# A retention layer and a channel mix on one core: scaled shifted rows on ScalarE instead of a difference on VectorE for four blocks, and a new hand-set order

## The chip, the core and the metric

The kernel runs on one core of one Trainium2 chip. A core has five engines that run side by side, each with its own queue of instructions taken strictly in order: PE (TensorE, matrix multiplication; PEld are its weight loads), DVE (VectorE), ACT (ScalarE), POOL (GpSimd, here used only to issue DMAs) and SP (SyncE, likewise). The metric is the device time of one execution in microseconds (us); less is better.

## The reference

Two layers, float32 in and out, batch B=4, heads H=8, tokens S=768, head size D=64, so the model width is 512; the hidden width of the second layer is 1024.

```
for t in range(S):
    state = gamma[None, :, None, None] * state + einsum('bhd,bhe->bhde', k[:, :, t], v[:, :, t])
    y[:, :, t] = scale * einsum('bhd,bhde->bhe', q[:, :, t], state)
...
x = y with the heads side by side; x_prev = x shifted by one token (a zero row first)
xk = mu_k * x + (1.0 - mu_k) * x_prev
xr = mu_r * x + (1.0 - mu_r) * x_prev
k = maximum(xk @ w_k, 0.0)
v = k * k @ w_v
r = 1.0 / (1.0 + exp(-(xr @ w_r)))
out = r * v
```

## The kernel before, in words

The 4 x 768 tokens are 12 blocks of 256 tokens, numbered 0 to 11; three of them make one batch row. Each block goes through two halves.

The first half is the retention in chunked form. `lq`, `lk`, `lv` load q, k and v of a block (`load`, lines 223 to 238); q and k are turned to fp16 on the way when POOL issues the load, while the very first loads of block 0 go over SP in fp32 and are cast on ACT (`cq`, `ck`). `vs` scales v on DVE (line 254). `Tq` and `Tk` transpose q and k on PE (line 273 for blocks 0 to 5, line 279 for blocks 6 to 11) and ACT copies them out of PSUM (`Eq`, `Ek`, line 242). `S` makes the scores on PE, `M` masks them on DVE (lines 348 and 355). `C` makes the block's part of the state on PE, `U` adds it up (DVE, line 420; the first of a batch row is a copy on ACT or DVE, lines 242 and 244), and `G` decays it into the next block (ACT as four instructions, line 425, or DVE as one, line 429). `I`, `Y` and `J` add the three parts of y on PE, and `D` writes y, transposed and scaled, into the tile `xT` on DVE (lines 508 and 515).

The second half is the channel mix. `dx` (line 530) takes on DVE the difference of the rows of `xT` and the rows shifted by one token, for the whole block: 1024 elements in each of 128 partitions. `X.n.w.j` (line 539) makes a quarter j of the mixed rows on DVE: difference times mu plus the shifted rows, once for the keys (w=0) and once for the gate (w=1), 256 elements for a single block and 512 for a pair. `K` multiplies the mixed rows by w_k on PE (line 563 for single blocks, line 553 for the pairs 3+4, 6+7 and 9+10), ACT takes the result out of PSUM (`Qa`, relu, line 572) and squares it (`Qb`, lines 580 and 584). `R` is the gate's product on PE (line 593) and `s` the sigmoid on ACT (line 599). `V` multiplies the squares by w_v (line 605), `O` multiplies by the gate on DVE (line 611), and `st` stores over SP.

The weights are loaded by POOL in halves: `wk.1` and `wk.0` (line 700), `wr` (line 703), `wv.0` and `wv.1` (line 707). `z.c` are matrix multiplications of zeros that fill PE's waits near the start (c // 4 of them in fp32, line 668, and c % 4 in fp16, line 675).

Nothing schedules this at run time. The string `ORDER` (lines 23 to 75) lists every piece in order, and each engine issues its own pieces in just this order. After `@` stand the PSUM banks of a piece, after `~` its engine or its DMA queue (v is DVE, a ACT, p POOL, s SP). A piece waits until what it reads has been written and until the bank or buffer that it writes has been read. Of the tiles for v there are four, so that the loads of blocks 0 to 3 wait for no one. DVE's first pieces in ORDER, once y of block 0 is there, are

```
D.0~v ... U.1.0 ... dx.0~v X.0.0.0 ... M.1.1~v M.1.0~v ... X.0.0.3 ... X.0.0.2 ... X.0.0.1 D.1~v
```

Of the kernel before, what the change touches and what calls it, by code (L numbers as in the profile page):

```python
# [28 lines left out]
z.4@2 S.1.1@01 lk.2~p I.1@45 S.1.0@23 M.1.1~v M.1.0~v lq.2~p Tq.2@6 Eq.2~a wk.1~p X.0.0.3 Tk.2@0
X.0.0.2 z.1@1 Y.1 J.1 X.0.0.1 D.1~v U.1.1 Ek.2~a z.1@2 S.2.1@01 S.2.0@23 K.0.2@6 dx.1~v K.0.3@4  # L30
Qa.0.3 Qa.0.2 wk.0~p z.2@5 K.0.1@7 Qa.0.1 K.0.0@5 Qb.0.2 X.0.1.0 X.1.0.2 lv.2~p Qa.0.0 Qb.0.1
X.1.0.3 wr~p X.1.0.1 X.1.0.0 K.1.2@4 lv.3~p G.1~a K.1.1@7 X.0.1.1 vs.2~v Qa.1.2 Qb.1.2 M.2.1~v
Qb.0.0 C.2@5 U.2.0 K.1.0@6 lq.3~p Qa.1.1 X.0.1.2 X.0.1.3 K.1.3@0 Qa.1.3 I.2@45 R.0.1@1 R.0.0@7
s.0.1 M.2.0~v Y.2 Qa.1.0 X.1.1.3 X.1.1.2 Qb.1.0 Tq.3@1 Eq.3~a J.2 X.1.1.0 X.1.1.1 R.1.0@6 s.0.0
lk.3~p Tk.3@1 vs.3~v D.2~v dx.2~v X.2.0.2 X.2.0.0 C.3@23 X.2.0.3 Ek.3~a s.1.0 X.2.0.1 lk.4~p
U.3.0~a R.1.1@0 lq.4~p s.1.1 Tk.4@1 S.3.1@45 S.3.0@67 Qb.1.1 Qb.1.3 U.3.1 lv.4~p Tq.4@0 Ek.4~a
Eq.4~a wv.0~p K.2.2@2 Qa.2.2 M.3.1~v K.2.0@3 Qa.2.0 G.3~a M.3.0~v K.2.3@1 vs.4~v Qb.0.3 S.4.1@45
S.4.0@67 M.4.0~v I.3@23 M.4.1~v Qa.2.3 lq.6~p lq.7~p K.2.1@0 Qb.2.0 Y.3 C.4@67 V.1.0.0@1 U.4.0
U.4.1 G.4~a I.4@45 J.3 Qa.2.1 D.3~v dx.3~v Y.4 V.1.1.0@6 Tq.7@23 J.4 D.4~v wv.1~p Qb.2.1
V.0.1.0@0 lk.6~p V.0.0.0@7 X.2.1.2 dx.4~v X.3.0.1 X.3.0.2 X.3.0.3 Eq.7~a V.1.1.1 X.3.0.0 V.0.0.1  # L40
O.0.0 Tk.6@45 Ek.6~a lq.5~p Tq.6@23 lv.5~p Qb.2.2 V.0.1.1 Eq.6~a V.1.0.1 O.1.0 K.3.6@4 K.3.1@5
Qb.2.3 lk.5~p K.3.0@7 Qa.3.6 Tq.5@4 Qa.3.1 Qa.3.0 vs.5~v C.5@5 X.2.1.1 Eq.5~a Tk.5@1 Ek.5~a
S.6@23 O.0.1 O.1.1 lk.7~p U.5.0 Tk.7@67 Ek.7~a X.2.1.0 I.5@45 M.6~v X.3.1.3 K.3.2@0 K.3.3@1
Qa.3.2 Qb.3.1 lv.6~p S.5.0@23 Qa.3.3 Qb.3.0 X.3.1.1 S.5.1@67 Qb.3.3 X.2.1.3 Qb.3.2 K.3.4@0
st.0.0 Qa.3.4 M.5.1~v lk.8~p K.3.5@1 Qa.3.5 R.2.1@6 lv.8~p lk.9~p s.2.1 M.5.0~v Y.5 S.7@23
Tk.8@01 Ek.8~a J.5 X.3.1.0 X.3.1.2 R.3.1@7 s.3.1 V.2.0.0@6 K.3.7@0 lv.7~p vs.6~v R.2.0@7 V.2.0.1
D.5~v M.7~v s.2.0 dx.5~v X.5.1.1 O.2.0 Qa.3.7 Qb.3.6 V.2.1.0@1 Tk.9@23 C.6@45 U.6.0~a Ek.9~a
lq.8~p Tq.8@67 Qb.3.7 X.5.0.3 V.2.1.1 vs.7~v R.4.0@0 Eq.8~a U.6.1 U.6.2 X.5.0.0 U.6.3 st.0.1
R.3.0@2 C.7@45 X.5.0.1 s.4.0 I.6@67 s.3.0 st.1.1 X.5.0.2 K.5.3@3 Qa.5.3 O.2.1 lq.10~p K.5.1@0
Qa.5.1 G.6~v X.5.1.3 V.3.0.0@1 U.7.0 U.7.1 U.7.2 st.2.1 I.7@23 Y.6 vs.8~v U.7.3 G.7~a lq.11~p  # L50
R.4.1@0 D.6~v V.4.1.0@4 lv.11~p C.8@67 Y.7 V.3.1.0@5 Qb.5.1 Qb.3.4 Qb.3.5 V.3.0.1 dx.6~v s.4.1
U.8.0 U.8.1 V.3.1.1 Qb.5.3 D.7~v U.8.2 V.4.1.1 dx.7~v X.6.0.1 X.6.0.3 V.4.0.0@7 K.5.0@6 X.5.1.2
X.6.0.2 Qa.5.0 V.4.0.1 Qb.5.0 K.5.2@0 X.6.0.0 Qa.5.2 Qb.5.2 X.6.1.2 lv.9~p K.6.7@6 Qa.6.7 st.2.0
st.1.0 O.4.1 O.3.0 K.6.0@2 Qa.6.0 lk.10~p O.4.0 O.3.1 st.3.1 K.6.4@0 S.8@67 I.8@23 Tk.10@45
Qa.6.4 K.6.1@1 Ek.10~a X.6.1.1 X.5.1.0 Qa.6.1 Qb.6.1 K.6.6@0 Qb.6.0 Qa.6.6 vs.9~v K.6.5@4 Qa.6.5
M.8~v R.5.1@1 Qb.6.6 Tq.10@67 Eq.10~a s.5.1 Y.8 Tq.11@45 Qb.6.7 lv.10~p vs.10~v X.6.1.3 Eq.11~a
D.8~v dx.8~v lq.9~p X.8.0.2 X.8.0.1 lk.11~p R.5.0@0 s.5.0 K.6.3@6 Qa.6.3 V.5.1.0@7 Tq.9@23
X.6.1.0 Eq.9~a S.10@45 M.10~v Qb.6.3 C.9@01 U.9.0~v st.3.0 U.9.1 V.5.1.1 K.6.2@6 Qa.6.2 R.6.1@2
s.6.1 U.9.2 R.6.0@3 s.6.0 I.9@45 U.9.3 O.5.1 X.8.0.3 S.9@01 M.9~v X.8.0.0 G.9~a C.10@67 U.10.0
U.10.1 Qb.6.2 vs.11~v R.7.1@2 s.7.1 V.5.0.0@3 Qb.6.5 st.4.1 Tk.11@01 Ek.11~a U.10.2 U.10.3  # L60
V.5.0.1 Qb.6.4 K.8.0@2 Qa.8.0 G.10~v I.10@01 Y.9 C.11@67 st.4.0 R.7.0@2 O.5.0 V.6.1.0@3 D.9~v
U.11.0 U.11.1 s.7.0 K.8.3@4 Qa.8.3 V.6.1.1 U.11.2 I.11@67 st.5.0 dx.9~v O.6.1 S.11@45 X.8.1.2
Y.10 V.7.1.0@2 M.11~v D.10~v dx.10~v X.9.0.3 X.9.0.2 X.9.0.1 V.7.0.0@3 Y.11 X.9.0.0 Qb.8.0
K.8.2@4 Qa.8.2 X.8.1.0 X.9.1.1 K.8.1@5 Qa.8.1 D.11~v V.6.0.0@0 V.7.0.1 V.6.0.1 K.9.3@1 K.9.7@5
Qa.9.7 X.8.1.1 V.7.1.1 X.8.1.3 dx.11~v K.9.2@4 O.7.0 Qb.8.1 Qb.9.7 O.6.0 Qa.9.3 st.5.1 Qa.9.2
X.11.1.0 Qb.8.3 X.11.0.3 K.9.1@5 K.9.4@6 st.7.0 Qa.9.1 Qb.9.1 R.8.0@1 s.8.0 V.8.1.0@3 Qb.9.2
X.9.1.0 K.9.0@0 Qa.9.0 Qb.8.2 X.9.1.2 Qb.9.3 K.9.6@1 Qa.9.6 Qb.9.6 O.7.1 st.7.1 K.9.5@7 Qa.9.5
V.8.0.0@0 X.11.0.2 X.11.0.1 Qb.9.0 X.11.0.0 K.11.3@2 K.11.0@1 Qa.11.3 st.6.1 R.8.1@5 V.8.1.1
X.11.1.2 Qa.9.4 st.6.0 X.9.1.3 R.9.1@2 R.10.1@4 R.10.0@6 V.8.0.1 O.8.0 s.8.1 K.11.1@5 Qb.9.4
s.10.0 V.9.0.0@7 V.9.1.0@0 Qa.11.1 Qb.11.1 O.8.1 Qb.9.5 Qb.11.3 Qa.11.0 st.8.1 K.11.2@6 Qa.11.2  # L70
V.10.1.0@5 Qb.11.2 Qb.11.0 V.9.1.1 R.9.0@1 X.11.1.3 s.9.0 X.11.1.1 V.9.0.1 O.9.0 st.9.0
V.11.0.0@6 s.10.1 s.9.1 O.9.1 st.9.1 V.10.0.0@1 V.10.1.1 O.10.1 st.8.0 st.10.1 V.11.0.1 R.11.0@0
s.11.0 O.11.0 V.10.0.1 R.11.1@7 s.11.1 O.10.0 st.10.0 Vc.11.1.1@0 Oc.11.1.1 Vc.11.1.0@6 st.11.0
sc.11.1.1~a Oc.11.1.0 sc.11.1.0~s
"""


# [687 lines left out]
```

## Time and profile before

| | us |
|---|---|
| median of 3 runs (156.35, 156.45, 157.85) | 156.45 |
| the profiled execution | 156.1 |
| its span in the trace | 154.3 |
| busy: PE / DVE / ACT / POOL | 147.3 / 128.1 / 99.1 / 55.2 |
| first matmul of the first `K` piece starts at | 20.45 |

A trace lists every instruction of one execution with its engine, its start and its length. The profile is a page drawn from it; further views of the same trace (groups by line and shape, stretches of time, instructions in order, DMA issues) are called answers here. Engines overlap, so a large busy share is no proof of a bound; the question is who waits for whom, and when. Matmuls are pipelined: the recorded length of one is longer than its distance to the next. The profiled execution took 1.8 us more than its span, for what lies before the first and after the last instruction.

### The profile page before, as it was taken

What the parts mean: (1) busy time and instruction counts of PE and PEld (TensorE: products, weight loads), DVE (VectorE), ACT (ScalarE), POOL (GpSimd) and SP (SyncE); (2) the same over time, 40 slices, a digit from 0 to 9 for tenths busy, and PEclk for the clock granted to TensorE, in tenths of its full rate; (3) what the DMA queues carried; (4) which work ended last, traced back from release to release, by engine and by line L of the source; (5) the groups of instructions that cost most, each with busy time, mean ns of one, the idle gap of its engine ahead of it and who ended that gap; (6) DMA issues with size and microseconds to landing.
All of it is one profiled execution on the core that took longest, in us unless ns stands there. A gap on an engine that the chain in (4) does not pass through costs nothing.

```text
span 154.3 us, 5316 instructions
## 1 busy us (share of the span) xinstructions
PE 147.3 (95%) x2316; PEld 84.2 (55%) x2316; DVE 128.1 (83%) x203; ACT 99.1 (64%) x182; POOL 55.2 (36%) x67
## 2 busy tenths in 40 slices
...
DMA  4999999999999999973999170000300015001435
GB/s 140 283 184 171 204 243 248 166 216 207 190 180 216 219 293 267 188 78 88 305 248 175 12 272 8 0 6 4 138 4 4 0 68 204 0 20 53 155 117 204
DMA packets 44903, 22.29 MB, mean 144 GB/s; under 512 B 36424, under 2 KB 40400, under 8 KB 44880
## 3 DMA queue, kind: packets, MB, share of 16 engines
...
q10 hardware_dynamic: 448, 0.32, 0.7%
...
## 4 chain that ended last, share of the span: by engine, by line
PE 42%; DVE 36%; issue 8%; POOL 6%; DMA 5%; ACT 3%; DVEq 0%; POOLq 0%
PE ps L605 13%; PE ps L553 9%; PE ps L593 8%; DVE xk L539 6%; PE ps L563 5%; DVE dx L530 5%; DMA q<-in_q_dram 5%; DVE xr L539 4%; DVE a L355 4%; DVE xT L515 3%; DVE vs L254 3%; DVE tg L420 3%; DVE os L611 2%; POOL k L231 2%; DVE xT L508 2%
## 5 line engine op out<-in xcount | busy, mean ns | idle before, releaser
L605 PE MATMUL ps<-wv,k2s 128*128 128x512 f16 x184 | 44.4, 380 | 0.0
L572 ACT ACTIVATE kr<-ps 128x512 f32<-128x512 f32 x48 | 27.8, 597 | 21.2 <-PE ps L563 11.7
L605 PEld LDWEIGHTS <-k2s 128*128 128x128 f16 x184 | 17.3, 98 | 18.8
L611 DVE SCALAR_TENSOR_TENSOR os<-ps,rs 128x512 f32<-128x512 f32 x23 | 15.1, 684 | 14.4 <-PE ps L605 7.9
L593 PE MATMUL ps<-wr,xr 128*128 128x512 f16 x96 | 23.9, 380 | 0.0
L231 POOL DMA_DIRECT2D v<-in_v_dram x22 | 19.8, 916 | 10.5 <-DVE vs L254 7.9
L563 PE MATMUL ps<-xk,wk 128*128 128x256 f16 x192 | 23.5, 273 | 0.0
L231 POOL DMA_DIRECT2D k<-in_k_dram x22 | 19.6, 905 | 10.5 <-DMA wk<-in_moe_w_k_dram 3.4
L553 PE MATMUL ps<-xk,wk 128*128 128x512 f16 x96 | 22.6, 379 | 0.8 <-DVE xk L539 0.8
L599 ACT ACTIVATE rs<-ps 128x512 f32<-128x512 f32 x24 | 14.1, 602 | 13.5 <-PE ps L593 9.4
L563 PEld LDWEIGHTS <-wk 128*128 128x128 f16 x192 | 18.2, 98 | 4.6 <-DMA wk<-in_moe_w_k_dram 0.5
L539 DVE SCALAR_TENSOR_TENSOR xr<-dx,mu,xT 128x256 f16<-128x256 f32 (+1 forms) x36 | 19.3, 566 | 0.0
L539 DVE SCALAR_TENSOR_TENSOR xk<-dx,mu,xT 128x256 f16<-128x256 f32 (+1 forms) x36 | 18.8, 567 | 0.2
L254 DVE TENSOR_TENSOR vs<-v,csm_sb 128x1024 f16<-128x1024 f32 x12 | 14.6, 1216 | 2.1 <-DMA v<-in_v_dram 2.1
L553 PEld LDWEIGHTS <-wk 128*128 128x128 f16 x96 | 9.0, 98 | 12.1 <-DVE xk L539 1.1
L242 ACT COPY kT<-ps 128x1024 f16<-128x1024 f16 (+1 forms) x13 | 12.2, 951 | 4.4 <-PE ps L279 3.3
L584 ACT ACTIVATE k2s<-kr 128x512 f16<-128x512 f32 x24 | 14.8, 632 | 0.2
L530 DVE TENSOR_TENSOR dx<-xT 128x1024 f32<-128x1024 f32 x12 | 14.6, 1219 | 0.2
L580 ACT ACTIVATE k2s<-kr 128x512 f16<-128x512 f32 x24 | 14.7, 629 | 0.1
L355 DVE TENSOR_TENSOR a<-ps,c_sb 128x1024 f16<-128x1024 f32 (+1 forms) x14 | 14.4, 1062 | 0.0
L242 ACT COPY qT<-ps 128x1024 f16<-128x1024 f16 (+1 forms) x13 | 12.3, 954 | 3.2 <-PE ps L273 2.9
L593 PEld LDWEIGHTS <-xr 128*128 128x128 f16 x96 | 8.7, 98 | 9.7
(67 smaller groups left out, 154.3 us busy)
## 6 DMA issues: line engine op xcount, KB each, us to landing
out_dram<-os SPq DMA_DIRECT2D x23, 256.0 KB, 2.6
v<-in_v_dram POOLq DMA_DIRECT2D x22, 256.0 KB, 7.0
...
q<-in_q_dram POOLq DMA_DIRECT2D x11, 256.0 KB, 7.8
wk<-in_moe_w_k_dram POOLq DMA_DIRECT2D x2, 512.0 KB, 10.2
wv<-in_moe_w_v_dram POOLq DMA_DIRECT2D x2, 512.0 KB, 10.0
...
```

The lines of the kernel that those rows point to most:

```text
L231: e.dma_start(out=dst[:, :, i * D : i * D + D], in_=src[:, i * P : i * P + P].rearrange("h p d -> p h d"),)
L242: e.copy(out=out, in_=in_)
L254: e.tensor_tensor(out=VS(n), in0=V32(n).rearrange("p h (i d) -> p i h d", i=2), in1=gks[:, int(half(n) or wide(n)), :, :, None].to_broadca ...
L355: nc.vector.tensor_tensor(out=a_full(n)[:, i, :, j0:j1], in0=pairs(banks("S", n, i, j0))[:, :, j0:j1], in1=(below if wide(n) else causal[: ...
L530: e.tensor_tensor(out=DX(k)[:, :, m * TM + t0 : m * TM + t1], in0=x[:, :, c + t0 : c + t1], in1=x[:, :, c - 1 + t0 : c - 1 + t1], op=ALU.s ...
L539: nc.vector.scalar_tensor_tensor(out=XM[w](k)[:, j, t0:t1], in0=DX(k)[:, j, t0:t1], scalar=mu[:, w * NCO + j : w * NCO + j + 1], in1=x[:, ...
L553: nc.tensor.matmul(banks("K", n, g), lhsT=wk16[:, co, g * P : g * P + P], rhs=XM[0](k)[:, co, :], start=(co == 0), stop=(co == NCO - 1),)
L563: nc.tensor.matmul(pz[:, i, :], lhsT=wk16[:, co, fo * P : fo * P + P], rhs=XM[0](k)[:, co, m * TM + t0 : m * TM + t1], start=(i == 0 and c ...
L572: nc.scalar.activation(out=kr, in_=banks("K", n, g, *u), func=AF.Relu)
L593: nc.tensor.matmul(banks("R", n, tb), lhsT=XM[1](k)[:, co, t : t + P], rhs=wr16[:, co, :], start=(co == 0), stop=(co == NCO - 1),)
L605: nc.tensor.matmul(banks("V", n, tb), lhsT=K2(n)[:, fo, tb * P : tb * P + P], rhs=wv16[:, fo, :], start=(fo == 0), stop=(fo == NFO - 1),)
L611: nc.vector.scalar_tensor_tensor(out=OS(2 * n + tb), in0=banks("V", n, tb), scalar=1.0 / (KSC * KSC), in1=RS(2 * n + tb), op0=ALU.mult, op ...
```

## The change

For blocks 0, 1, 2 and 5 (`PARTED`) there is no `dx`. Instead ACT makes, for each w and j, the shifted rows times one minus mu (`ax.n.w.j`, eight instructions of 128 x 256 per block, 32 in all) into the buffer that held the difference, and `X` becomes rows times mu plus that. One minus mu (`nu`) is made once by one more small ACT instruction. The other blocks keep `dx`. The whole of `ORDER` is new: among much else, the loads of v go over SP instead of POOL (all but that of block 10), so that POOL's queue begins with k and q of block 0, then q and k of blocks 1 and 2, then `wk.1` and `wk.0`; `G.1`, `G.3` and `G.9` go from ACT to DVE and `G.6` from DVE to ACT; `U.3.0` goes from ACT to DVE; the fillers are `z.8`, `z.2`, `z.3`, `z.1`, `z.2`, `z.4` in place of `z.12`, three of two, two of four and three of one unit. `WKP` is 2, so the weights' halves stay; `whole` gives the same blocks as before.

```diff
+PARTED = (0, 1, 2, 5)
+WKP = 2
 ORDER = """
-lk.0.0.2~s gy.0 lq.0.2.4~p lv.0~p lq.0.0.2~s lk.0.2.4~p ck.0.0.2~a z.12@6 Tk.0.0.2@0 mu
-Tq.0.2.4@1 cq.0.0.2~a z.2@6 Tq.0.0.2@2 Ek.0.0.2~a vs.0~v Eq.0.0.2~a z.2@6 S.0.1.0.2@45
...
+gy.0 lk.0.2.4~p lq.0.0.2~s cq.0.0.2~a z.8@7 Tq.0.0.2@0 lq.0.2.4~p lk.0.0.2~s ck.0.0.2~a z.2@1
+Tk.0.0.2@1 Tk.0.2.4@2 Tq.0.2.4@3 lv.0~s vs.0~v Eq.0.0.2~a Ek.0.0.2~a S.0.0.0.2@45 lq.1~p lk.1~p
+Ek.0.2.4~a lv.1~s M.0.0.0.2~v Eq.0.2.4~a z.3@6 S.0.1.2.4@67 M.0.1.2.4~v C.0@01 mu Tq.1@3
+S.0.1.0.2@45 U.0.0~a U.0.1 I.0@67 M.0.1.0.2~v S.0.0.2.4@01 gy.1~a M.0.0.2.4~v lq.2~p Tk.1@2 Y.0
+vs.1~v z.1@4 C.1@45 Eq.1~a mt@3 Ek.1~a G.0~a me S.1.0@01 D.0~v ax.0.0.3 ax.0.1.1 ax.0.1.3
+ax.0.0.0 ax.0.0.2 lk.2~p U.1.0 z.2@2 I.1@23 S.1.1@67 ax.0.0.1 M.1.0~v Tk.2@0 M.1.1~v X.0.0.3
+X.0.0.0 Tq.2@1 Eq.2~a Y.1 Ek.2~a J.1 X.0.0.1 z.4@6 S.2.1@67 D.1~v ax.0.1.0 ax.1.0.3 S.2.0@01
+wk.1~p wk.0~p X.0.0.2 K.0.3@2 U.1.1 X.1.0.3 ax.1.0.1 ax.1.0.2 K.0.2@3 X.1.0.2 ax.1.0.0 X.1.0.0
+ax.1.1.1 lv.2~s wr~p ax.1.1.0 lv.3~s X.1.0.1 K.1.3@5 K.1.2@4 Qa.0.3 ax.1.1.2 Qa.0.2 K.0.0@3
+ax.1.1.3 Qb.0.3 Qa.1.3 Qa.1.2 K.1.1@2 X.0.1.1 M.2.1~v X.1.1.0 lk.3~p K.0.1@4 lq.3~p lk.4~p
+ax.0.1.2 Qb.0.2 Qa.0.0 G.1~v Qb.0.0 X.0.1.3 Qa.1.1 Qb.1.1 vs.2~v C.2@5 X.1.1.1 Qb.1.3 lq.4~p
+K.1.0@3 X.0.1.0 X.1.1.2 Qa.0.1 U.2.0 X.0.1.2 I.2@67 R.0.1@2 Qa.1.0 X.1.1.3 vs.3~v R.1.1@4 s.0.1
...
+    nu = const.tile([P, 2 * NCO], F32, name="nu")
...
+    def kept(n, w, j):
+        return DX(place[n][0])[:, j, w * TM : w * TM + TM]
+
+    def keep(e, n, w, j):
+        x, c = col(n)
+        nc.scalar.activation(
+            out=kept(n, w, j), in_=x[:, j, c - 1 : c - 1 + TM], func=AF.Copy,
+            scale=nu[:, w * NCO + j : w * NCO + j + 1],
+        )
...
+        if n in PARTED:
+            nc.vector.scalar_tensor_tensor(
+                out=XM[w](k)[:, j, 0:TM], in0=x[:, j, c : c + TM],
+                scalar=mu[:, w * NCO + j : w * NCO + j + 1], in1=kept(n, w, j),
+                op0=ALU.mult, op1=ALU.add,
+            )
+            return
...
         nc.scalar.copy(out=mu, in_=banks("mt")[:, 0 : 2 * NCO])
+        if PARTED:
+            nc.scalar.activation(out=nu, in_=mu, func=AF.Copy, scale=-1.0, bias=1.0)
```

More of the change, by code (lines that the diff above doesn't have):

```diff
@@ L29 @@
[L29 to L74, printed above, removed]
+gy.0 lk.0.2.4~p lq.0.0.2~s cq.0.0.2~a z.8@7 Tq.0.0.2@0 lq.0.2.4~p lk.0.0.2~s ck.0.0.2~a z.2@1
+Tk.0.0.2@1 Tk.0.2.4@2 Tq.0.2.4@3 lv.0~s vs.0~v Eq.0.0.2~a Ek.0.0.2~a S.0.0.0.2@45 lq.1~p lk.1~p
@@ new lines @@
+ax.1.1.1 lv.2~s wr~p ax.1.1.0 lv.3~s X.1.0.1 K.1.3@5 K.1.2@4 Qa.0.3 ax.1.1.2 Qa.0.2 K.0.0@3
+ax.1.1.3 Qb.0.3 Qa.1.3 Qa.1.2 K.1.1@2 X.0.1.1 M.2.1~v X.1.1.0 lk.3~p K.0.1@4 lq.3~p lk.4~p
+ax.0.1.2 Qb.0.2 Qa.0.0 G.1~v Qb.0.0 X.0.1.3 Qa.1.1 Qb.1.1 vs.2~v C.2@5 X.1.1.1 Qb.1.3 lq.4~p
+K.1.0@3 X.0.1.0 X.1.1.2 Qa.0.1 U.2.0 X.0.1.2 I.2@67 R.0.1@2 Qa.1.0 X.1.1.3 vs.3~v R.1.1@4 s.0.1
+Tk.3@5 Ek.3~a C.3@23 M.2.0~v Y.2 lv.4~s J.2 U.3.0~v U.3.1 Tq.3@2 s.1.1 D.2~v Eq.3~a ax.2.0.3
+R.1.0@3 R.0.0@4 ax.2.0.1 G.3~v S.3.0@01 S.3.1@67 X.2.0.3 X.2.0.1 wv.0~p ax.2.0.0 ax.2.0.2 s.1.0
@@ new lines @@
+X.2.0.0 Qb.1.2 X.2.0.2 lk.6~p Tk.4@5 M.3.0~v lq.6~p Ek.4~a Tq.4@3 K.2.3@2 wv.1~p K.2.0@5 M.3.1~v
+K.2.1@0 Eq.4~a S.4.0@67 Qa.2.3 Qb.1.0 Qa.2.0 vs.4~v S.4.1@23 M.4.1~v K.2.2@1 s.0.0 Qb.0.1 Qa.2.2
+ax.2.1.2 Qb.2.0 ax.2.1.1 I.3@45 lq.7~p Y.3 C.4@23 V.0.0.0@1 M.4.0~v U.4.0 U.4.1 I.4@67 J.3
+lv.5~s G.4~a D.3~v Y.4 V.1.1.0@3 Tk.6@45 Qa.2.1 J.4 lq.5~p V.1.0.0@0 Qb.2.1 ax.2.1.0 V.0.1.0@2
+V.0.1.1 dx.3~v Ek.6~a D.4~v dx.4~v X.3.0.2 X.3.0.3 X.3.0.0 V.1.0.1 X.3.0.1 Tq.7@45 Tq.6@67
+Qb.2.2 Eq.6~a O.1.0 lk.5~p Qb.2.3 X.3.1.0 V.0.0.1 O.0.0 lk.8~p V.1.1.1 K.3.1@6 Eq.7~a vs.5~v
@@ new lines @@
+O.0.1 K.3.2@7 lk.7~p Qa.3.1 S.6@45 M.6~v lv.6~s O.1.1 ax.2.1.3 Qa.3.2 Tq.5@1 Eq.5~a Tk.5@7
+Ek.5~a C.5@6 U.5.0 X.2.1.1 X.3.1.1 K.3.3@0 K.3.0@1 X.2.1.3 Qa.3.3 Qa.3.0 K.3.6@7 Qb.3.3 Qa.3.6
+lq.11~p I.5@45 S.5.0@23 M.5.0~v S.5.1@01 M.5.1~v K.3.4@6 Qb.3.2 Qa.3.4 lv.7~s K.3.5@7 K.3.7@6
+lq.8~p Qb.3.1 X.2.1.2 Qa.3.5 Qb.3.5 Qb.3.6 Qa.3.7 Y.5 Tk.7@23 Ek.7~a Tk.8@01 Ek.8~a J.5 X.2.1.0
+lq.9~p vs.6~v lv.10~p D.5~v ax.5.1.3 R.2.1@7 V.2.1.0@6 vs.7~v st.0.0 Qb.3.7 R.2.0@4 s.2.0 st.1.0
+X.3.1.2 ax.5.0.1 S.7@23 C.6@01 X.3.1.3 U.6.0~a V.2.1.1 R.3.1@4 M.7~v V.2.0.0@5 U.6.1 V.2.0.1
```

36 lines of the change are left out of this document (30 added, 6 removed).

## The prediction

> **What bounds the kernel now.** First the page's busy shares, then ten-microsecond stretches, to see which engine is full and when.
>
> ```profile
> span 154.3 us, 5316 instructions
> PE 147.3 (95%) x2316; PEld 84.2 (55%) x2316; DVE 128.1 (83%) x203; ACT 99.1 (64%) x182; POOL 55.2 (36%) x67
> ...
> DMA  4999999999999999973999170000300015001435
> ```
> ```profile
> core 0: us, PE busy (x) PEld busy (x) DVE busy (x) ACT busy (x) POOL busy (x), PEclk, DMA share, GB/s
> 0.00:10.00 10.00, 8.36 (x98) 4.10 (x99) 4.63 (x16) 5.34 (x9) 8.96 (x15) 1.00 1.00 209
> 10.00:20.00 10.00, 8.88 (x188) 5.59 (x190) 9.83 (x15) 6.26 (x13) 7.56 (x9) 1.00 1.77 185
> 20.00:30.00 10.00, 10.00 (x104) 7.50 (x103) 10.00 (x17) 6.95 (x16) 5.53 (x7) 1.00 1.39 225
> 30.00:40.00 10.00, 9.97 (x175) 6.91 (x173) 9.58 (x14) 9.57 (x18) 7.53 (x10) 1.00 1.66 201
> ...
> 110.00:120.00 10.00, 9.61 (x189) 5.55 (x188) 9.83 (x14) 2.31 (x4) 0.00 (x0) 1.00 0.06 20
> 120.00:130.00 10.00, 10.00 (x51) 4.80 (x49) 9.55 (x18) 8.30 (x16) 0.00 (x0) 1.00 0.23 86
> 130.00:140.00 10.00, 10.00 (x62) 5.80 (x60) 2.08 (x4) 5.60 (x12) 0.00 (x0) 1.00 0.12 45
> ```
>
> Two engines are full at once. DVE works 9.6 to 10 of every 10 us from 10 to 130, and PE nearly all the time from 20 to 151. But PE's lengths hide waits, since matmuls are pipelined. So I took the distance from each piece's first matmul to the next piece's, piece by piece through ORDER, and let the low quarter of each kind (0.863 us for four matmuls of 512, 0.873 for `K` of a single block) stand for its work. That gives 131.1 us of work, 9.6 of fillers and 9.4 of stretch. From the first `K` (20.45) to the last matmul's end (151.2) PE has 123.2 us of work, 0.6 of filler and 7.0 of stretch, 2.8 of it in ten gaps of 0.16 to 0.56. So what can be won is the time before 20.45 and those 7.0 us, no more. From 119 on there is no stretch at all. The chain of waits says the same: DVE pieces from 27 to 85, PE pieces from 119 to the end.
>
> What holds the start? The answers for single instructions show loads.
>
> ```profile
> 17.24 0.64 PE L273 MATMUL ps<-c_sb,q 128*64 128x128 f16 x16 [0.70 <-DMA q<-in_q_dram]
> ...
> 20.45 1.92 PE L563 MATMUL ps<-xk,wk 128*128 128x256 f16 x16
> ```
> ```profile
> 20.09 0.88 POOL L231 DMA_DIRECT2D k<-in_k_dram  x1 [1.35 <-DMA wk<-in_moe_w_k_dram]
> 23.04 0.88 POOL L231 DMA_DIRECT2D k<-in_k_dram  x1 [2.07 <-DMA wk<-in_moe_w_k_dram]
> ```
>
> PE waits at 17.24 for q of block 2. POOL's two waits end when the halves of w_k land, near 20.0 and 23.0, and the first `K` starts at 20.45. The page's DMA row stands at nine tenths from 4 to 62 us. The beginning is bound by loads and by DVE together.
>
> **The change part by part.** Prices:
>
> ```profile
> L530 DVE TENSOR_TENSOR dx<-xT 128x1024 f32<-128x1024 f32 x12 | 14.6, 1219 | 0.2
> ...
> L425 ACT ACTIVATE tg<-t,csm_sb 128x64 f16<-128x64 f32 x24 | 6.4, 348 | 3.0 <-DVE t L420 3.0
> ...
> L686 ACT ACTIVATE gy_sb<-gy_sb,csm_sb 128x128 f32<-128x128 f32 x4 | 1.3, 391 | 0.0
> ...
> L580 ACT ACTIVATE k2s<-kr 128x512 f16<-128x512 f32 x24 | 14.7, 629 | 0.1
> ```
> ```profile
> v<-in_v_dram POOLq DMA_DIRECT2D x22, 256.0 KB, 7.0
> ...
> k2s<-in_k_dram SPq DMA_DIRECT2D x1, 256.0 KB, 3.2
> ```
>
> *DVE.* Four `dx` go: 4 x 1.22 = 4.9 us. `X` keeps its shape and price (0.48). Two decays more than before (0.42 each, line 429) and `U.3.0` (0.42) come over: +1.3. Net -3.6 of 128.1. Nearly all would count if DVE alone set the pace, but PE is full beside it.
>
> *ACT.* Line 686 has the form of `ax` (copy, scale from a column, fp32 from and to SBUF) at half its length. Busy time over count gives 0.27 for 64 elements (line 425) and 0.32 for 128, so 0.43 for 256. Bounds: 0.32 (it can't cost less than half of itself) and 0.63 (line 580, twice as long). I take 0.43: 32 x 0.43 = 13.8 us, between 10.2 and 20.2. `nu` adds 0.2; two decays (1.06 each) and `U.3.0` (0.37) leave. Net +11.5, so ACT goes from 99 to about 111 us, 71% of the span. Each `X` of these blocks now also waits for ACT, where before only DVE's own queue came first.
>
> *Where this lies.* Distances between starts, summed along both orders: behind 27 us of PE's work DVE has had to do 32.2 instead of 35.8 us and ACT 33.1 instead of 26.7; behind 53, DVE 60.7 instead of 62.2 and ACT 55.7 instead of 45.6; behind 99, DVE 103.9 instead of 111.7 and ACT 83.6 instead of 73. So DVE is ahead of need by 1.5 to 8 us more than now, and ACT is crowded only early: its row has 7.0 and 9.6 busy in 20 to 40, and 14 of the 32 `ax` come there, 6 just before.
>
> *Queues.* 21 of 23 issues of v (0.9 us each) leave POOL, 55 to 36 us. In front of `wk.1` POOL then has eight issues, and starts it near 8.3 instead of 10.74. On SP, four q and k loads and stores are joined by v; v of blocks 0 to 3 finds free buffers, so SP issues 2 MB at once and `lv.4` as soon as `vs.0` is done. Behind a waiting `lv.7` stands the first store; four buffers of results cover it, and no wait of that kind is due before 50 us.
>
> *The loads, in source bytes.* Before, 4.0 MB (q and k of 0 to 2, v of 0 and 1) lie up to 17.24; from about 2 us that is 0.26 MB a us; w_k then takes 2.9 us a half, 0.34. I take 0.30. In the new order k of block 1 needs 2.5 MB plus what SP has pushed in between of v 1 to 3 (0 to 1.5): 10.3 to 15.3 us, half way 12.8, against 12.69 now. q and k of block 2 need 3.5 plus the same: 13.7 to 18.7, middle 16.2 (now 17.24). `wk.1`: 17 to 22, middle 19.5 (now 20.0). I take the middles, since nothing in this trace has the two queues full at once.
>
> Here a rule bears. A load of 256 KB on SP landed 3.2 us after its issue, one of v on POOL 7.0; by that row v would cost the pool's loads nothing any more. The Trainium skill, "DMA: Bandwidth & Descriptors", section "Issuing engines are not separate DMA queues", says that DMAs of all issuers run on the same 16 engines and interleave, and that issuing from several saves only issue time. By the row, block 2 is there at 13.7; by the rule the sum of bytes counts, up to 18.7. The row of nines speaks for the rule.
>
> *First `K` to S.4.0.* From block 2's landing (16.2): two transposes 0.95, two copies on ACT 1.9, two scores 0.5: `K.0.3` near 19.5. DVE gives the same: y of block 0 from 12.3 (12.86 now; its first scores no longer wait for `z.12`), then `U.1.0` 0.4, two masks 2.3, three `X` 1.2, and after a short wait for PE y of block 1 and one `X`, 1.6: near 19.4. Then ACT is late: five `ax` (2.15) behind the copies, so `K.1.3` waits 0.75 and starts at 22.0; later `K.1.0` waits 0.3 and `R.1.1` 0.55 for relus that stand behind `ax` (ACT runs without a gap there). `R.1.1` comes at 29.3 with 16.15 us of PE work done; before, PE had done as much at 29.6. The same walk to `S.4.0` gains another 0.2. Head: -0.5, with both ends of the loads -1.0 to +2.0.
>
> *Rest.* From `S.4.0` to the end PE has 5.4 us of stretch now. DVE's lead should remove about a third of the 2.4 us in long gaps there: -0.7, bounds 0 and, if the small ones wait for DVE too, -3.3. Fewer fillers cost nothing while PE waits for loads. The tail (last two pieces, 3.1 us to the end) is unchanged.
>
> Sum: 156.1 - 0.5 - 0.7 = 154.9 for the profiled execution; the median of the runs shown is 0.35 above it: 155.3.
>
> **The rivals.**
>
> *Slower: v in front of everything.* SP's 2 MB of v, not needed before 24, take turns with q, k and w_k. It decides once v of 2 and 3 is in before block 2 (5.0 MB, 18.7): then `K.0.3` comes at 22, ACT's crowd follows at once, and `R.1.1` stands 2.0 us later instead of 0.3 earlier. With the late gain: 155.3 + 2.5 = 157.8, up to 159. For it: the DMA row. Against it: SP's part can be smaller than a fair share.
>
> *ACT becomes the bound.* If `ax` takes 0.63 instead of 0.43, the 14 of the stretch without a gap cost 2.8 us more: 155.3 + 2.8 = 158.1. Against it: the row of line 686.
>
> *More than forecast.* The stretch of 7.0 us is mostly waiting for DVE, in small pieces, and DVE's lead takes half of it: 155.3 - 2.6 = 152.7. For it: DVE at 9.6 to 10 and the chain of waits from 27 to 85. Against: matmul pieces of other shapes follow each other there, and changes of shape could cost as much with nobody waiting. With v beside the other loads at no price (the row above), DVE still holds `K.0.3` at about 19.3, so this case alone is worth 0.3.
>
> **How the numbers follow.** Forecast 0.43 (own range 154.0 to 156.6), more than forecast 0.24, v in front 0.23, ACT 0.10. About 1% (1.6 us) is what a measurement of this kernel can tell from no change: faster is below 154.9, slower above 158.0. Faster: 0.23 of the third rival and 0.14 of the forecast's lower part, 0.37. Slower: half of v in front (0.12), part of ACT (0.06) and 0.08 for both together or stores held up on SP, 0.26. The rest, 0.37, is within. Range: 152.4 (third rival's far end) to 159.0 (the slower ones), leaving 0.1 on each side.
>
> **What would show it.** Right: DVE busy near 124.5, ACT near 111; an `ax` group at about 0.49 each and 13 to 14 us in all; `K` first at 19 to 20; ACT without gaps from 20 to 30; PE's last stretch again without a gap. Wrong: k of block 1 landing after 14 or `wk.1` after 21; PE waiting for `ax` or relus beyond 40 us; gaps ahead of masks or `vs` for v; stores waiting on SP.

## The result, and the profile after

The changed kernel takes 170.88 us (median of 4 runs, 170.86 to 171.93); the kernel before took 157.15 beside it (median of 4, 156.35 to 158.53). The ratio is 1.088, with an interval of 1.079 to 1.096; ratios here leave out runs more than 1.5% above the fastest of the same kernel, which belong to a slower state. The profiled execution of the changed kernel took 171.93 with a span of 170.2; its last store took 1.3 us longer than that of the execution before (the other three runs are 1.05 us shorter than this one), so 14.5 of the 15.9 us between the spans remain to be explained.

The page after: span, busy shares, granted clock, DMA row, and the two queues (q0 is POOL's, q1 SP's).

```profile
span 170.2 us, 5312 instructions
...
PE 153.2 (90%) x2311; PEld 87.6 (52%) x2311; DVE 125.4 (74%) x202; ACT 110.9 (65%) x206; POOL 36.3 (21%) x46
...
PEclk9955555999996999999999999999999999999999
DMA  5999999999999999999999090401100410220072
...
q0 software_dynamic: 38176, 9.18, 55.3%
q1 hardware_dynamic: 26352, 12.45, 32.9%
```

ACT came out as forecast (111), DVE nearly so: 2.7 us less than before, where 3.6 less (124.5) was forecast. What changed is the stretch in which the DMA row stands at nine tenths: it ends at 94 us instead of 62, for the same 22.29 MB. The two queues before:

```profile
q0 software_dynamic: 39920, 14.95, 75.2%
q1 hardware_dynamic: 4512, 6.69, 11.9%
```

So 5.77 MB of v are 21840 packets on SP (264 bytes each), and POOL has 1744 packets fewer for the same 5.77 MB (3.3 KB each).

Ten-microsecond stretches after: DVE's column was 9.6 to 10 from 10 on.

```profile
10.00:20.00 10.00, 7.71 (x148) 5.02 (x148) 5.51 (x8) 4.45 (x11) 3.25 (x4) 0.50 1.64 165
20.00:30.00 10.00, 8.89 (x110) 5.15 (x111) 7.10 (x11) 6.60 (x17) 3.49 (x4) 0.51 1.32 188
30.00:40.00 10.00, 9.88 (x104) 7.37 (x98) 9.66 (x18) 9.94 (x22) 2.52 (x3) 1.00 1.53 170
40.00:50.00 10.00, 6.10 (x129) 3.96 (x128) 7.76 (x12) 6.24 (x11) 3.56 (x5) 1.00 1.50 173
50.00:60.00 10.00, 10.00 (x132) 6.61 (x127) 4.63 (x7) 7.12 (x15) 3.31 (x4) 0.83 1.46 176
60.00:70.00 10.00, 9.61 (x197) 5.11 (x198) 9.83 (x13) 6.58 (x12) 3.50 (x4) 1.00 2.09 168
```

From 10 to 30 and from 40 to 50 no engine is full: everybody waits. From 50 to 60 PE is full by its recorded lengths, but 3.4 us of that (50.2 to 53.6) ran at half clock. The answers for single instructions of PE say for what (the last bracket is the wait ahead of a piece and what ended it).

```profile
17.58 0.96 PE L278 MATMUL ps<-c_sb,k 128*64 128x128 f16 x14 [1.68 <-DMA k<-in_k_dram]
...
24.83 0.96 PE L278 MATMUL ps<-c_sb,k 128*64 128x128 f16 x14 [1.11 <-DMA k<-in_k_dram]
...
30.34 1.92 PE L585 MATMUL ps<-xk,wk 128*128 128x256 f16 x16
...
42.96 0.64 PE L278 MATMUL ps<-c_sb,q 128*64 128x128 f16 x16 [0.91 <-DMA q<-in_q_dram]
...
47.74 0.58 PE L278 MATMUL ps<-c_sb,k 128*64 128x128 f16 x14 [1.58 <-DMA k<-in_k_dram]
...
49.58 0.64 PE L278 MATMUL ps<-c_sb,q 128*64 128x128 f16 x16 [1.25 <-DMA q<-in_q_dram]
```

Line 278 transposes q and k: k of block 1 (17.58), k of block 2 (24.83), q of block 3 (42.96), k and q of block 4 (47.74, 49.58). The first `K` starts at 30.34, not at 20.45. DMA issues, with the median from issue to landing in us as the last number, after and then before (v's 7.0 before stands in the prediction):

```profile
v<-in_v_dram SPq DMA_DIRECT2D x20, 256.0 KB, 13.0
k<-in_k_dram POOLq DMA_DIRECT2D x23, 128.0 KB, 11.8
q<-in_q_dram POOLq DMA_DIRECT2D x11, 256.0 KB, 14.9
wk<-in_moe_w_k_dram POOLq DMA_DIRECT2D x2, 512.0 KB, 21.4
```
```profile
k<-in_k_dram POOLq DMA_DIRECT2D x23, 128.0 KB, 7.4
q<-in_q_dram POOLq DMA_DIRECT2D x11, 256.0 KB, 7.8
wk<-in_moe_w_k_dram POOLq DMA_DIRECT2D x2, 512.0 KB, 10.2
```

To put a place to the time, I call *lag* the start of a piece minus PE's work ahead of it in its own order, by the same lengths as in the prediction. V.2.1.1 is a piece that all orders have at about the same place; "v on POOL" is the experiment of that name below.

| lag, us | before | after | v on POOL |
|---|---|---|---|
| at the first `K` | 12.5 | 22.4 | 14.4 |
| at V.2.1.1 (68 to 81 us) | 16.5 | 31.9 | 18.6 |
| at the last `V` | 19.9 | 34.4 | 25.2 |

Of 14.5 us, 9.9 are lost before the first `K` and 5.5 more up to V.2.1.1 (3.7 are PE's waits for q of block 3, 0.91 at 42.96, and for k and q of block 4). Behind that the changed kernel loses 2.5 where the kernel before lost 3.4.

### The profile page after: what moved, and what is told of

Same layout as the page of the kernel before. It is cut to its first block, busy times and chain, and to the rows that moved or that the text cites. A ratio compares the mean times of both kernels' runs of the same rounds, so it can differ in the third digit from the quotient of the medians.

```text
span 170.2 us, 5312 instructions
## 1 busy us (share of the span) xinstructions
PE 153.2 (90%) x2311; PEld 87.6 (52%) x2311; DVE 125.4 (74%) x202; ACT 110.9 (65%) x206; POOL 36.3 (21%) x46
## 2 busy tenths in 40 slices
DMA packets 64999, 22.29 MB, mean 131 GB/s; under 512 B 56904, under 2 KB 61904, under 8 KB 64976
## 4 chain that ended last, share of the span: by engine, by line
PE 60%; DMA 24%; ACT 7%; POOL 4%; issue 2%; DVE 0%; ACTq 0%; POOLq 0%
PE ps L627 22%; DMA wk<-in_moe_w_k_dram 12%; DMA q<-in_q_dram 12%; PE ps L575 11%; PE ps L585 10%; PE ps L615 8%; PE ps L284 2%; POOL k L236 2%; PE ps L447 2%; POOL q L241 1%; ACT dx L545 1%; ACT rs L621 1%; ACT k2s L602 1%; PE ps L468 1%; ACT kT L247 1%
## 5 line engine op out<-in xcount | busy, mean ns | idle before, releaser
L633 DVE SCALAR_TENSOR_TENSOR os<-ps,rs 128x512 f32<-128x512 f32 x23 | 15.3, 684 | 14.9 <-ACT rs L621 13.3
L585 PE MATMUL ps<-xk,wk 128*128 128x256 f16 x192 | 25.0, 285 | 0.0
L575 PE MATMUL ps<-xk,wk 128*128 128x512 f16 x96 | 22.4, 379 | 0.5 <-issue 0.5
L621 ACT ACTIVATE rs<-ps 128x512 f32<-128x512 f32 x24 | 13.8, 598 | 13.3 <-PE ps L615 13.3
L585 PEld LDWEIGHTS <-wk 128*128 128x128 f16 x192 | 19.0, 102 | 4.6
L360 DVE TENSOR_TENSOR a<-ps,c_sb 128x1024 f16<-128x1024 f32 (+1 forms) x14 | 14.6, 1068 | 7.6 <-PE ps L337 6.2
L259 DVE TENSOR_TENSOR vs<-v,csm_sb 128x1024 f16<-128x1024 f32 x12 | 14.6, 1218 | 4.4 <-DMA v<-in_v_dram 4.4
L575 PEld LDWEIGHTS <-wk 128*128 128x128 f16 x96 | 9.1, 98 | 11.2 <-issue 0.8
L545 ACT ACTIVATE dx<-xT,nu 128x256 f32<-128x256 f32 x32 | 14.6, 504 | 0.2
L602 ACT ACTIVATE k2s<-kr 128x512 f16<-128x512 f32 x24 | 14.4, 626 | 0.2
L241 POOL DMA_DIRECT2D q<-in_q_dram x12 | 10.5, 878 | 14.4 <-PE ps L278 3.6
L561 DVE SCALAR_TENSOR_TENSOR xr<-dx,mu,xT 128x512 f16<-128x512 f32 (+1 forms) x20 | 12.4, 638 | 0.1
L561 DVE SCALAR_TENSOR_TENSOR xk<-dx,mu,xT 128x512 f16<-128x512 f32 (+1 forms) x20 | 11.7, 640 | 0.1
```

The source lines that it names most:

```text
L545: nc.scalar.activation(out=kept(n, w, j), in_=x[:, j, c - 1 : c - 1 + TM], func=AF.Copy, scale=nu[:, w * NCO + j : w * NCO + j + 1],)
L561: nc.vector.scalar_tensor_tensor(out=XM[w](k)[:, j, t0:t1], in0=DX(k)[:, j, t0:t1], scalar=mu[:, w * NCO + j : w * NCO + j + 1], in1=x[:, ...
L575: nc.tensor.matmul(banks("K", n, g), lhsT=wk16[:, co, g * P : g * P + P], rhs=XM[0](k)[:, co, :], start=(co == 0), stop=(co == NCO - 1),)
L585: nc.tensor.matmul(pz[:, i, :], lhsT=wk16[:, co, fo * P : fo * P + P], rhs=XM[0](k)[:, co, m * TM + t0 : m * TM + t1], start=(i == 0 and c ...
L602: nc.scalar.activation(out=k2s[:, n % 3 : n % 3 + 2, g, :], in_=kr, func=AF.Square,)
L621: nc.scalar.activation(out=RS(2 * n + tb), in_=banks("R", n, tb), func=AF.Sigmoid, scale=1.0 / KSC)
```

## The experiments

Theory: SP's v goes packet by packet in turn with POOL's loads, so that q, k and w_k land late, and that is nearly the whole loss. Rivals: the new order or `ax` costs it; the halved clock costs it.

**v back on POOL** (`e1_v_on_pool`: the changed kernel, `lv` at the same places in ORDER)

```diff
-... lv.0~s vs.0~v ... lv.1~s ... lv.2~s wr~p ... lv.3~s ...
+... lv.0~p vs.0~v ... lv.1~p ... lv.2~p wr~p ... lv.3~p ...
```

> The changed kernel with all loads of v back on POOL, at the same places in the order. Theory (v on SP is the cause: its packets take turns with those of q, k and w_k): first K piece at 19.5 to 22 us, TensorE clock at full after 10 us, 154.5 to 158 us. Rival (the new order is slow by itself, through the pieces that ACT has taken over): at least 165 us. Rival (the short fillers leave TensorE cold, whatever the loads do): half clock from 10 to 30 us as now, 160 us or more.

Measured: 162.04 us (ratio to before 1.034, 1.025 to 1.042). 8.8 of 13.7 us are gone, so v on SP is the larger part of the loss; 154.5 to 158 was expected, and about 5 us stay. Its packets are those of before, its loads land nearly as fast as before, the first `K` starts at 22.34, and the clock is halved only from 17.0 to 20.4:

```profile
k<-in_k_dram POOLq DMA_DIRECT2D x23, 128.0 KB, 7.7
q<-in_q_dram POOLq DMA_DIRECT2D x11, 256.0 KB, 8.9
wk<-in_moe_w_k_dram POOLq DMA_DIRECT2D x2, 512.0 KB, 10.2
```
```profile
22.34 6.86 PE L585 MATMUL ps<-xk,wk 128*128 128x256 f16 x56
```

**The same alone in the old order** (`e4_before_v_on_sp`: the kernel before, all `lv` but block 10's on SP)

```diff
-... lv.0~p ... lv.1~p vs.1~v ... lv.2~p ... lv.3~p
+... lv.0~s ... lv.1~s vs.1~v ... lv.2~s ... lv.3~s
```

> The kernel before with its loads of v moved from POOL to SP (all but block 10), nothing else. Theory (v on SP is the cause): first K at 27 to 31 us instead of 20.45, 165 to 171 us. Rival (new order or ACT pieces are the cause): 155 to 159 us.

Measured: 169.03 against 157.08, one run. The one edit costs 12 us, though neither `ax` nor the new order is in it. PE in this kernel:

```profile
24.47 1.06 PE L273 MATMUL ps<-c_sb,q 128*64 128x128 f16 x16 [4.81 <-DMA q<-in_q_dram]
...
29.08 1.92 PE L563 MATMUL ps<-xk,wk 128*128 128x256 f16 x16
```

The piece that waited 0.70 us for q of block 2 at 17.24 now waits 4.81.

**Two buffers for v instead of four** (`e2_v_ring_two`), so that SP can't run ahead by more than two blocks. In this kernel v of block 8 is loaded over v of block 10, which stands ahead of it in ORDER and is read later; the work and its waits are those of two buffers.

```diff
-    V32 = ring("v32_", 4, [H, 2 * D], F32)
+    V32 = ring("v32_", 2, [H, 2 * D], F32)
```

> The changed kernel with two buffers for v instead of four, so that the loads of v of block 2 and later wait on SP for the scaling of a block two earlier. Theory, by running ahead: v of blocks 2 and 3 no longer comes before q, k and w_k, first K near 24 to 27 us, 161 to 166 us. Theory, by price alone (each packet of v costs a turn whenever it comes): little gained, 168 to 171 us. Rival (order or fillers): unchanged, 170 to 172 us.

Measured: 170.78, one run. The first `K` came at 26.62, 3.7 earlier, as running ahead would have it, and the time is that of price alone. What was gained was given back later: PE still waits for k and q of block 4 (1.16 and 1.58, at 42.46 and 44.62), and the lag grows from 27 to 33.5 between 83 and 115 us, which I did not follow further. Running ahead is a part of the delay of the first `K`, not the whole of it.

**v in pieces of 512 bytes** (`e3_v_512_bytes`)

```diff
-"lv": load(v, V32, True)
+"lv": load(v, V32, False)
```

> The changed kernel with v of blocks 1 to 11 loaded in pieces of 512 bytes instead of 256 on SP; the bytes are the same but half as many packets; v's tokens come to other places, so the output is not the reference's. Theory by packets (a packet of 256 bytes takes the DMA engines as long as one of 512): v takes half the time, first K near 24 to 26 us, 160 to 165 us. Theory by bytes: no difference, 169 to 172 us.

Measured: 169.46, one run, and the first `K` at 32.22. The theory by packets fell. The time lies in the range of the theory by bytes, but v did come faster: with half as many packets it ran still further ahead (v of block 4 had landed at 23.1), in front of block 2 and w_k; the gain came only later (lag 32.4 at the end).

What the queues do can be counted in the packet records of the trace (changed kernel, per microsecond):

```
            POOL packets  KB    SP packets  KB
26 to 27    148           147   150         38
28 to 29    171           150   171         44
30 to 31    226           127   230         58
32 to 33    291           104   291         73
```

In these microseconds, and in all from 24 to 34, both queues give one packet in turn, whatever its size. In others of the same stretch POOL gives more (711 to 193 from 11 to 12, 709 to 179 from 41 to 42); why SP falls behind there was not followed. The Trainium skill, "DMA: Bandwidth & Descriptors", section "Queues, rings and completion order", says that an engine takes turns between the queues that have work, a packet at a time, where a packet is a group of descriptors; the table agrees, if what the trace records as a packet is that. Fitted by least squares over 6 to 45 us (before, after, v on POOL, and the experiment above), a packet takes on one of the 16 engines: POOL's 128 bytes of k 13.7 ns, 256 of q 22, 1024 of a weight 80, 4096 of v 207 to 229; SP's 256 of v 25.7, and 32 where it is 512. So 256 KB of v cost 0.8 to 0.9 us of all engines from POOL (64 packets, each 207 to 229 ns, on 16 engines) and 1.6 from SP (1024 packets of 25.7): about twice the price. And more of it is in front. When k of block 2 had landed (24.8 us), SP had read v of block 0 (1024 packets of 512 bytes) and 4889 packets of 256 of blocks 1 to 3: 1.7 MB, by the prices above 9.9 us of all engines. In v on POOL 1.0 MB of v, blocks 0 and 1, was in front of it: 3.3 to 3.7 us. These 6 us are most of the 7.5 that k of block 2 is later (24.8 for 17.3); about 4 of them are the price, 2 the larger amount. For `wk.1` it is 7 of 8.9 us (28.8 for 19.9).

**Where the rest is** (`e5_pool_as_before`: new order, but POOL's own sequence and its place among the needs as before; `e8_pool_as_before_dx`: the same with `dx` instead of `ax`)

```diff
-gy.0 lk.0.2.4~p lq.0.0.2~s ... lq.0.2.4~p ... lv.0~p ... lq.1~p lk.1~p ... lv.1~p ... lq.2~p
+lq.0.2.4~p lv.0~p lk.0.2.4~p lv.1~p lk.1~p lq.1~p lk.2~p lq.2~p wk.1~p wk.0~p lv.2~p wr~p lv.3~p lq.3~p
...
-PARTED = (0, 1, 2, 5)
+PARTED = ()
```

(The second pair of lines is in the second kernel alone.)

> The changed kernel with all weights, k, q and v of all blocks (but the two first loads over SP) on POOL in the sequence of the kernel before; the pieces of the four computing engines stay in the new order. Theory (the queues alone made it slow; in the run with v on POOL at the new places the last 3 us were lost because POOL stood for 7.6 us at a load of v with q and k of blocks 9 to 11 behind it): first K at 20 to 22 us, 155 to 159 us. Rival (the new order or the ACT pieces cost the rest): 161 to 164 us, as with v on POOL at the new places.

> As the run with POOL's loads in the sequence of the kernel before, but with the difference on DVE for all blocks instead of the scaled rows on ACT (each dx where the first ax of its block stood). Theory (the ACT pieces are worth what DVE is relieved by, where DVE is the bound): 1 to 4 us slower than that run. Rival (the ACT pieces cost as much in ACT's waits): within 1 us of it, or faster.

Measured: 162.03 (1.035, 1.029 to 1.041) and 166.39 (1.061, 1.054 to 1.068). So about 5 us stay even when POOL gives every load as before; the theory (155 to 159) fell, the rival held. But they are not the same 5 us as in v on POOL: here the first `K` came at 24.57 (20 to 22 expected), and PE waits for q of block 1, which stands early in the new order and late in POOL's old sequence:

```profile
13.48 1.07 PE L272 MATMUL ps<-c_sb,q 128*64 128x128 f16 x16 [2.27 <-DMA q<-in_q_dram]
```

Order and sequence of loads go together, and no run parts them fully. Within that order `ax` is 4.4 us faster than `dx`, just above the 1 to 4 expected; the order was made for `ax`, so this is no price of `ax` by itself.

**`ax` in the old order** (`e6_ax_in_old_order`: for blocks 0, 1, 2, 5, a few pieces ahead of their `X`; `e11_ax_block5_old_order`: for block 5 alone)

```diff
-... Tq.1@1 Eq.1~a dx.0~v X.0.0.0
+... Tq.1@1 Eq.1~a ax.0.0.0 ax.0.0.3 ax.0.0.2 ax.0.0.1 X.0.0.0
```

> The kernel before with the four differences of blocks 0, 1, 2 and 5 replaced by the 32 scaled shifted rows on ACT, nothing moved otherwise (each ax a few pieces ahead of its X). Theory of the forecast (DVE is relieved by 4.9 us, ACT has room over the whole but not between 20 and 40 us): 154 to 158 us, the gain in DVE and the waits behind ACT near equal. Rival (ACT is the bound once it has the 32 pieces): 159 to 163 us.

> The kernel before with scaled rows on ACT for block 5 alone, the other blocks with the difference on DVE. Theory (the pieces cost where ACT is crowded, from 15 to 45 us, and block 5 comes near 70 us): within 1 us of before, 155.5 to 157.5 us. Rival (each X that waits for ACT costs, wherever it stands): 2 us for eight of the 32 pieces, 158 to 159 us.

Measured: 164.22 (1.049, 1.042 to 1.056), slower than either theory had it, and 156.95 (0.999, 0.995 to 1.003), as expected. Waits of DVE in the first of them, 10 to 60 us, and two stretches (columns as above, ACT the fourth busy time):

```profile
DVE xk L549 <- ACT dx L539: 5.5, 3, 3.4
DVE t L419 <- ACT tg L241: 2.4, 1, 2.4
```
```profile
20.00:30.00 10.00, 7.48 (x86) 5.81 (x79) 6.44 (x12) 8.52 (x20) 5.49 (x7) 1.00 1.40 225
30.00:40.00 10.00, 7.72 (x112) 4.67 (x110) 8.23 (x15) 9.03 (x19) 6.92 (x9) 1.00 1.66 202
```

ACT has 8.5 to 9 busy of 10 and DVE stands behind it. Moving the work to ACT is thus worth nothing by itself: 7.8 us dearer where the order is left alone, free for block 5, where ACT has room, and 4.4 cheaper than `dx` in an order made for it, which is itself slower than the old one.

**The clock** (`e7_more_fillers`: changed kernel with more `z`; the diff shows only some of them)

```diff
-... Tk.0.0.2@1 Tk.0.2.4@2 Tq.0.2.4@3 ... Tk.1@2 ... Tk.2@0 ... Tq.4@3
+... Tk.0.0.2@1 z.4@6 Tk.0.2.4@2 z.4@6 z.3@6 Tq.0.2.4@3 ... z.4@2 z.4@2 Tk.1@2 ... z.4@0 Tk.2@0 ... z.12@3 Tq.4@3
```

> The changed kernel with more matmuls of zeros ahead of the pieces that wait for loads (before the transposes of blocks 0, 1, 2 and of q of block 4, and before the scores of block 2). Theory (half clock is a consequence of PE's idling and costs about 1.6 us at the K pieces of block 2 and 1 us or so in the head): clock near full from 10 us on, 167 to 169.5 us. Rival (the clock is the main loss): 160 to 164 us. Rival (the clock costs nothing, loads hold PE anyway): 170 to 172 us.

Measured: 171.75, one run, beside 171.93 and 170.88. The clock row and the first `K`:

```profile
PEclk9999995999999999999999999999999999999998
```
```profile
30.60 3.67 PE L580 MATMUL ps<-xk,wk 128*128 128x256 f16 x32
```

Full speed up to 25.5 us (half from 25.5 to 28.9), and `K` no earlier. The theory (167 to 169.5) fell. As far as one run tells, the half clock is a result of waiting, not its cause.

**The other 5 us** (`e9_v10_later`: `lv.10` behind `lk.10`; `e10_head_mended`: also Y.0 and D.0 ahead of vs.1 and C.1)

```diff
-lq.9~p vs.6~v lv.10~p D.5~v
+lq.9~p vs.6~v D.5~v
...
-... lk.10~p Tk.10@01 Ek.10~a
+... lk.10~p lv.10~p Tk.10@01 Ek.10~a
...
-M.0.0.2.4~v lq.2~p Tk.1@2 Y.0 vs.1~v z.1@4 C.1@45 Eq.1~a mt@3 Ek.1~a G.0~a me S.1.0@01 D.0~v
+Eq.1~a M.0.0.2.4~v lq.2~p Y.0 D.0~v mt@3 me Tk.1@2 vs.1~v z.1@4 C.1@45 Ek.1~a G.0~a S.1.0@01
```

> The run with v on POOL at the new places, with the load of v of block 10 moved behind those of k of blocks 9, 10 and 11, q of 10 and v of 8 and 9, so that POOL doesn't stand 7.6 us at it before the rest can be issued. Theory (that wait cost PE the 3 us between 74 and 94 us): 158 to 160 us. Rival (the new order or ACT loses these 3 us anyway): 161.5 to 163 us.

> As the run with v of block 10 later, and at the start y of block 0 and its copy into xT come ahead of the transposes of k of block 1 and of the scaling of v of block 1, as in the order before. Theory (the other 2 us are lost because the new order lets y of block 0 wait for loads of block 1, which it expects early): first K at 20.5 to 21.5 us instead of 22.3, 156.5 to 158.5 us. Rival (ACT's crowded start sets the first K pieces): first K stays at 22 us, within 0.5 us of that run.

Measured: 162.88 (160.30 to 164.94; ratio 1.026, 1.012 to 1.040) and 162.73 (1.035, 1.027 to 1.044). The first can't tell its two expectations apart. In the second both fell. POOL's stop went from v of block 10 to k of block 11 (8.34 us), and the first `K` of the second came at 23.62: C.0 and C.1 wait for vs there (1.43, 0.90). On POOL v of block 0 stands third, behind k and q of block 0, and v of block 1 behind q and k of block 1.

Besides, kernels of this family stop at one place. PE, in v on POOL:

```profile
81.18 0.41 PE L372 MATMUL ps<-vs,k 64*64 64x64 f16 x23
83.84 0.19 PE L372 MATMUL ps<-vs,k 64*64 64x64 f16 x1 [2.25 <-issue]
83.85 0.45 PE L284 MATMUL ps<-c_sb,q 64*64 64x64 f16 x32
84.23 4.34 PE L627 MATMUL ps<-wv,k2s 128*128 128x512 f16 x12
```

"issue" says that PE waits for nothing that the trace shows. The stop ends at the 1376th weight load of the trace in every one of them (the expectation below calls it the 1379th), and the trace has packets of 16 KB on a queue named instruction:

```
kernel                stop ends    16 KB packet read     stop, us
v on POOL             83.84        81.38 to 82.44        2.25
POOL as before        85.89        83.52 to 84.48        2.25
the same with dx      89.13        86.73 to 87.69        2.36
v of block 10 later   85.75        83.31 to 84.52        2.25
head mended           86.02        83.27 to 84.61        1.98
two buffers for v     92.63        90.28 to 91.23        1.96
```

Each stop ends 1.2 to 1.4 us after the packet. (In the last kernel the trace names ACT for the wait, but that instruction had ended 0.5 us before.) There are 18 such packets, and weight loads and matmuls together are 4622; 256 a packet. So PE's own program seems to come late. The changed kernel bears that out from the other side: its packet is read by 92.70, and it passes the same weight load at 94.18, 1.48 us later, without a stop. In v on POOL the clock is halved from 85.2 to 88.7, behind the stop, and twelve matmuls take 4.34 instead of 2.8 us: 3.8 us together.

**Long products ahead of short ones** (`e12_long_ahead_of_short`: v on POOL, one step moved)

```diff
-Y.7 X.5.1.1 D.7~v C.8@23 G.7~a U.8.0 U.8.1 Tq.10@67 Eq.10~a V.3.1.0@1 V.4.1.1 O.4.1 ax.5.1.2 V.3.1.1 U.8.2
+V.3.1.0@1 V.4.1.1 V.3.1.1 Y.7 X.5.1.1 D.7~v C.8@23 G.7~a U.8.0 U.8.1 Tq.10@67 Eq.10~a O.4.1 ax.5.1.2 U.8.2
```

> The kernel with v's loads back on POOL's queue (162.0 us) with one step moved: V.3.1.0, V.4.1.1 and V.3.1.1 (twelve 128x512 products, 2.8 us of TensorE) ahead of Y.7, C.8 and Tq.10 instead of behind them. Five kernels in the new order (v on POOL, POOL as before, dx in place of ax, v of block 10 later, head mended) stand still for 2.0 to 2.4 us at the same weight load, the 1379th, ahead of Tq.10, with nothing in the trace that they wait for, and each time the stop ends 1.2 to 1.4 us after a packet of 16 KB of the queue named instruction has been read (81.38 to 82.44, stop until 83.84). Theory 'the program arrives late': between the 1251st and the 1379th weight load nearly all products are 64x64 ones, so TensorE runs through its 16 KB of program in 3.4 us while POOL's burst of loads keeps the DMA engines full. With 2.8 us of long products in that stretch the stop shrinks to under 0.5 us (or lies elsewhere, at the 1379th weight load again, if the packet comes as late as 4 us more), the half clock behind it (1.5 us at 85 to 88) goes, and the time is 158 to 160 us. Rival 'a buffer or a load': Tq.10 or C.8 wait for something of their own (q of block 10, banks 6 and 7); the stop stays just ahead of Tq.10, whatever the number of its weight load, TensorE has only moved the long products forward, and the time stays 161 to 163 us. Rival 'VectorE': with Y.7 2.8 us later VectorE starves and the gain is lost there, 161 to 163 us, with no stop of TensorE at Tq.10.

Measured: 161.19 (1.029, 1.021 to 1.036). PE, then DVE:

```profile
84.35 0.29 PE L372 MATMUL ps<-vs,k 64*64 64x64 f16 x11
84.98 0.28 PE L372 MATMUL ps<-vs,k 64*64 64x64 f16 x11 [0.34 <-issue]
...
86.97 1.02 PE L615 MATMUL ps<-wr,xr 128*128 128x512 f16 x4 [1.43 <-DVE tg L425]
```
```profile
84.64 1.49 DVE L513 TENSOR_TENSOR xT<-ps,gy_sb 128x512 f32<-128x512 f32 x2 [3.33 <-PE ps L447]
```

The stop shrank from 2.25 to 0.34 us and moved back to the middle of C.8, twelve weight loads earlier in the pieces, as the theory of the program has it; it still ends 1.4 us after its packet (82.27 to 83.59). The rival for Tq.10 falls. The time hardly followed, because the other rival is right too: DVE, with Y.7 later, stood idle for 3.33 us, PE then waited 1.43 for it, and the clock was halved all the same. Its time was above the 158 to 160 of the theory and within the rival's range. Why the packet starts late there stays open: POOL's loads keep q0 busy around it (102% of 16 engines' time from 74 to 87 us by the packets' durations), but so they do in the changed kernel, which doesn't stop (120% from 82 to 95). No kernel here beats the one before.

## Why the prediction was wrong, point by point

*The bound now* was read rightly: the beginning hangs on loads and DVE. That the DMA row at nine tenths from 4 to 62 leaves no room was seen, and not priced.

*DVE:* -3.6 forecast, -2.7 measured (128.1 to 125.4). *ACT:* 111 forecast, 110.9 measured; an `ax` 0.49 forecast, 0.504 measured; 14.6 us in all against 13.8. The row of line 686 was the right one to go by. In the page after:

```profile
L545 ACT ACTIVATE dx<-xT,nu 128x256 f32<-128x256 f32 x32 | 14.6, 504 | 0.2
```

*Queues:* POOL 36.3 busy as forecast. No instruction of DVE waited for a buffer of results; by the trace only POOL's issue of v of block 10 waited for a store (7.27 us, up to 78.32), and no run shows what that cost.

*The loads, in source bytes:* this step failed. "I take 0.30" MB a us priced v alike on both queues; measured, the source bytes came at 0.21. k of block 1 landed at 17.5 (forecast 12.8, end 15.3), q and k of block 2 at 20.3 and 24.8 (16.2, end 18.7), wk.1 at 28.8 (19.5, end 22): behind the far ends too, since these were sums of bytes. For from SP v came in 256-byte packets at about twice the engine time. "I take the middles", half of the v of blocks 1 to 3 in front, was right for k of block 1 (SP had read 0.71 of 1.5 MB by then) and too low later (1.2 by 24.8, 1.3 by 28.8). That is the smaller error: at 0.30 the amounts that came would have put k of block 2 at 17.6 and wk.1 at 21.5. v on POOL takes back 8.8 us, and v on SP alone costs the old order 12. The price per byte was an unknown cost that the prediction did not put down as one: no row of the page before shows packet sizes for v on SP.

*First K to S.4.0:* what cost time there was not foreseen at all: k and q of block 4 and q of block 3 (PE waits 3.7 us). Whether ACT's crowd would have cost what was forecast can't be seen behind these waits.

*Rest:* -0.7 forecast. From V.2.1.1 on the changed kernel lost 0.9 less than before. That the size fits is luck: the stretch is another one, and why it lost less was not shown. With v on POOL the same stretch loses 3.2 more than before, and the stop of PE with the half clock behind it is 3.8.

*The rivals.* "v in front of everything" was the right mechanism with the wrong size: 2.5 us, since it put block 2 at 18.7, at the same 0.30 MB a us; it is worth 8.8 in the new order and 12 in the old one. "ACT becomes the bound" did not happen in the changed kernel, but the old order shows it (5.5 us of waits of DVE for `ax`). "More than forecast" fell: even without v on SP the new order is 5 us behind. Of these no single cause is shown.

*The row of 3.2 us* for a load on SP, weighed against the rule of the Trainium skill ("DMA: Bandwidth & Descriptors", section "Issuing engines are not separate DMA queues") that the DMAs of all issuers interleave on 16 engines: the rule held, in the packet counts above. That load was issued at 0.74 us, before POOL's first at 1.24, and landed at 3.98, when little else ran, so its row could not price twenty under load.
